# Attention and feed-forward on one Trainium2 core: three-product half-precision arithmetic replaced by an expansion about each batch's mean value

## The chip, the cores and the metric

The kernel runs on one core of one Trainium2 chip. The metric is the device time of one execution in microseconds (us), the median over runs. Engines are named as in the profile: PE (matrix products), PEld (its weight loads), DVE (vector), ACT (scalar and table functions), POOL (GpSimd) and SP (here only the queue from which all transfers are issued).

## The reference

```python
B, N, C = 4, 12288, 128            # kv: (4, 384, 32, 128), w_sr: (128, 128)
kv_pool = kv.reshape(B, 96, 4, 8, 4, C).mean(axis=(2, 4))     # 768 keys a batch, means of 16 places
k = v = kv_pool.reshape(B, 768, C) @ w_sr
s = (q @ k.transpose(0, 2, 1)) / sqrt(C)
a = exp(s - s.max(-1)); a /= a.sum(-1) + 1e-9
x = (a @ v).reshape(49152, 128)
h = x @ w_in                        # 128 -> 2048
out = (h - tanh(h)) @ w_out         # 2048 -> 128
```

All arrays are float32 but the two feed-forward weights, which are float64 and are handed over as pairs of 32-bit words. q is drawn with a standard deviation of 0.8, kv with 0.1 and w_sr with 0.05.

## The kernel before

The 49,152 tokens are cut into 96 groups of 512 (`NG` = 24 groups for each of 4 batches). Features lie on the 128 partitions, tokens on the free axis. Every piece of work is an operation of a `Plan`: it has a step (a priority), an engine, an assumed duration, and the tiles that it reads and writes. `Plan.run` places all operations by a list schedule and emits them in that order, so each engine's instruction order is fixed when the kernel is built. Tables of numbers (`SHIFT`, `FIRST`, `EARLY`) move the steps of each kind of operation. An added dependency, commented as "the shared way", puts a POOL instruction behind the DVE instruction emitted just ahead of it.

- `weights_in`, `weights_out` and `words_of` turn the float64 words into float32, and then into high and low half-precision parts (`wih`, `wil`, `woh`, `wol`, `wos`).
- `keys` makes a batch's 768 keys. For batch 0 PE sums the 16 places by accumulating products; for later batches DVE reduces chunks `kc` in pieces (L541).
- `attention` for a group: q is split in a high and a low half, PE multiplies three pairs of halves into `s` (L738, four blocks of 128 tokens by 768 keys), DVE takes the row maximum (L746), ACT the exponential (L752) and a half-precision copy (L757), POOL the remainder `a` (L761). A transposing DMA turns the weights, PE multiplies three pairs again (L819, 18 products of 512 columns), and DVE divides by the sum of the row (L833), which went through DRAM.
- `feed_forward` for a group: eight units `u` of 256 features. For each, PE makes `h` in three half-precision products for each of two halves (L860 to L862), ACT takes tanh (L888) and its square (L891), DVE multiplies `h` by it (L894). POOL, or ACT for unit 3, takes the high half `gh` (L898, L902), DVE the low half `gl` (L905), and PE goes back in three products for each half (L866 to L868) into the bank `acc`. So tanh itself is evaluated at one point of a quadrature for each value, and h - tanh(h) comes from it.
- `is_small` checks limits under which this holds. If they don't, a branch at the end (`ffn_any`) computes everything again for any inputs.
- `busy` fills pauses at the start with spare products (L1159).

PSUM has eight banks of 512 float32: `s` takes two, `h` two pairs, `x` and `acc` one each.

Of the kernel before, what the change touches and what calls it, by code (L numbers as in the profile page):

```python
# [9 lines left out]
F32 = mybir.dt.float32  # L10
I32 = mybir.dt.int32
U32 = mybir.dt.uint32
U16 = mybir.dt.uint16
BF16 = mybir.dt.bfloat16
F16 = mybir.dt.float16
# [4 lines left out]
DRAM = bass.MemoryType.DRAM  # L20
# [5 lines left out]

SMALL = 0.04
NODE = math.sqrt(0.6)
WEIGHT = math.sqrt(5.0 / 9.0)

# [9 lines left out]

LIFT = 15


SCORE = 2.0**20
MOST = 65000.0

LOW = 4096.0

LARGE, RAISE, LEAST = 30, 37, 2.0**11

ON_ACT = (3,)  # L60

IN_AFTER, OUT_AFTER = (0, 2, 4, 6), (8, 10, 12, 14)


SYNC = mybir.DependencyInfo(mybir.DependencyClass.Sync, mybir.DependencyReason.DATA)


class Plan:

    HOP = 0.1
    OWN = {"DVE": 0.16, "ACT": 0.02}

    SHIFT = {
        "divide": -1.31, "exps": -1.11, "forth": 0.78, "fro": 3.81, "g_high": 0.18,  # L80
        "g_low": 0.61, "inverse": -0.62, "largest_score": -1.19, "largest_x": -0.1,
        "load_row": 1.75, "load_words": -0.23, "pool": 14.11, "q_high": 0.01, "q_low": 0.58,
        "result": -1.34, "scores": 0.17, "square": -0.97, "store": -0.67, "store_row": 2.86,
        "store_x": -1.51, "tanh": -0.49, "turn_weights": -0.28, "values": 0.65,
        "weight_high": 3.21, "weight_low": 0.56, "x_high": 0.74, "x_low": -6.78,
    }

    FIRST = {
        "add": -1.15, "copy": -2.95, "copy_row": -3.44, "diagonals": 2.15, "divide": 2.2,
        "exps": -0.48, "forth": 3.21, "fro": 5.77, "g_high": 5.63, "g_low": -0.58, "high": 1.2,  # L90
        "inverse": 1.95, "keys_wide": -3.05, "largest": 1.58, "largest_score": -0.7,
        "largest_share": -0.86, "largest_x": -0.04, "load_q": -0.86, "load_row": 0.3,
        "load_words": 2.23, "low": 0.38, "lower": 1.13, "pool": 12.09, "q_high": -1.54,
        "q_low": 1.38, "result": 0.16, "rows": 0.22, "scaled": -0.24, "scores": -4.96,
        "scores_wide": -1.06, "shares": 2.06, "shift": -0.18, "size": -0.23, "sizes": 3.78,
        "small": 3.27, "square": -0.09, "squares_q": 3.77, "store": 0.64, "store_row": 3.52,
        "store_x": 1.91, "sum_of_rows": -1.91, "sums": 5.55, "tanh": 1.16, "times": 0.34,
        "top": -0.25, "turn_weights": 3.35, "upper": -0.01, "values": 1.54, "values_high": 0.24,
        "weight_high": -0.71, "weight_low": 3.46, "whole": 0.51, "within": 0.38, "x_high": -1.77,
        "x_low": -3.93,  # L100
    }
    UNTIL = 28
    SOON_FIRST, FIRST_US = 0.111, 150.0

    EARLY = {"attention 0": -5.7, "attention 1": 10.0, "attention 2": 2.9, "attention 3": 2.0, "weights_in": 3.9, "weights_out": 7.1}
    KEEP_US = 75.0
    SOON = 0.153
    TURN = 0.19

    def __init__(self, tc):  # L110
        self.tc = tc
        self.ops, self.tiles, self.rings = [], {}, {}
        self.names, self.later, self.emitted = {}, [], set()

    def tile(self, key, tag, bufs, make):
        ring = self.rings.setdefault(tag, [])
        self.tiles[key] = dict(make=make, ring=ring, place=len(ring), bufs=bufs, by=[], ap=None)
        ring.append(key)
# [7 lines left out]
    def op(self, step, engine, us, emit, reads=(), writes=(), late=0.0, port=False, dma=0.0,  # L126
           name=None, after=None, wide=False, dram=None):

        i = len(self.ops)
        kind = getattr(emit, "func", emit).__name__
# [1082 lines left out]
```

## Time and profile before

| | |
|---|---|
| median of 3 runs | 2829.96 us (2829.03 to 2830.73) |
| span of the profiled execution, first to last instruction | 2827.8 us |
| what lies around that span, against the median | 2.2 us |
| matrix products, weight loads | 13444 each |
| DVE, ACT, POOL instructions | 3201, 3311, 1057 |
| DMA | 285.02 MB, mean 101 GB/s |
| granted clock of PE, mean over the span | 1.000 |

The page gives the share of the span in which each engine was busy, then the same in 40 slices, then groups of instructions with the mean duration of one. A duration of DVE or ACT reaches a little into the next instruction of the same engine, so two neighbours' starts are closer together than the duration says. A matrix product's duration contains the way through the array, so products that follow one another start much closer together than their durations. For both the timeline, which gives each start, is read beside the groups.

### The profile page before, as it was taken

The numbers are of one execution on the slowest core, as the hardware profiler recorded it, in microseconds if no ns is written. First come the engines' busy times: TensorE is split into PE (matmuls) and PEld (weight loads), VectorE is DVE, ScalarE is ACT, GpSimd is POOL, SyncE is SP. The second block draws the span as 40 slices with busy tenths as digits, with TensorE's granted clock in tenths as the row PEclk, the third lists the DMA queues.
The fourth block names the chain that finished last, engine by engine and source line by source line (L and its number), as shares of the span: only waits on it lengthen the run. The fifth ranks groups of instructions, "written<-read, shape, count | busy, mean of one in ns | idle before, by whom it ended". The sixth has DMA issues, their size and how long they took to land. (4 is left out here: it accounts for less than half of the span.)

```text
span 2827.8 us, 39636 instructions
## 1 busy us (share of the span) xinstructions
PE 2791.7 (99%) x13444; PEld 1318.1 (47%) x13444; DVE 2693.8 (95%) x3201; ACT 2606.8 (92%) x3311; POOL 1327.6 (47%) x1057
## 2 busy tenths in 40 slices
PE   7999999999999999999999999999999999999998
PEld 4444444444444444444444444444444444444443
DVE  7999999999999999999999999999999999999998
ACT  7999999999999999999999999999999999999987
POOL 1545444444445454444445454444445454545442
PEclk9999999999999999999999999999999999999999
DMA  8534455554444445555434444555444444444440
GB/s 235 107 73 99 94 114 118 109 119 88 91 94 94 93 94 120 118 117 101 98 85 94 93 94 101 116 118 115 103 94 89 91 93 92 94 94 94 90 83 24
DMA packets 700324, 285.02 MB, mean 101 GB/s; under 512 B 629072, under 2 KB 656848, under 8 KB 700112
## 3 DMA queue, kind: packets, MB, share of 16 engines
q1 hardware_dynamic: 700112, 282.41, 46.8%
q8 instruction: 107, 1.75, 0.3%
q14 instruction: 105, 0.86, 0.1%
HBM read 79.23 MB, written 50.52 MB: 46 GB/s over the span
## 5 line engine op out<-in xcount | busy, mean ns | idle before, releaser
L898 POOL TENSOR_SCALAR gh<-gg 128x1024 f16<-128x1024 f32 x672 | 701.2, 1043 | 1344.0 <-DVE gl L905 1038.0
L894 DVE SCALAR_TENSOR_TENSOR gg<-h,by_batch,t 128x1024 f32<-128x1024 f32 x768 | 978.0, 1274 | 23.7 <-ACT t L891 17.3
L905 DVE SCALAR_TENSOR_TENSOR gl<-gh,gg 128x1024 f16<-128x1024 f16 x768 | 969.2, 1272 | 1.5 <-POOL gh L898 0.2
L888 ACT ACTIVATE t<-h,by_batch 128x1024 f32<-128x1024 f32 x768 | 849.6, 1106 | 63.4 <-PE h L862 55.2
L891 ACT ACTIVATE t<-t 128x1024 f32<-128x1024 f32 x768 | 811.4, 1056 | 21.0
L761 POOL TENSOR_TENSOR a<-e,a 128x768 f16<-128x768 f32 x380 | 625.8, 1647 | 147.0 <-ACT a L757 74.4
L860 PE MATMUL h<-x,wih 128*128 128x512 f16 x1536 | 582.7, 379 | 11.5 <-DVE gg L894 11.0
L868 PE MATMUL acc<-gl,wos 128*128 128x512 f16 x1536 | 582.1, 379 | 1.3 <-DVE gl L905 1.3
L861 PE MATMUL h<-x,wih 128*128 128x512 f16 x1536 | 582.1, 379 | 0.9 <-DVE x L840 0.9
L866 PE MATMUL acc<-gh,woh 128*128 128x512 f16 x1536 | 582.1, 379 | 0.3 <-POOL gh L898 0.2
L867 PE MATMUL acc<-gh,wol 128*128 128x512 f16 x1536 | 582.1, 379 | 0.0
L862 PE MATMUL h<-x,wil 128*128 128x512 f16 x1536 | 582.1, 379 | 0.0
L819 PE MATMUL x<-at,vv 128*128 128x512 f16 x1728 | 466.0, 379 | 2.2 <-DVE xf L833 1.7
L752 ACT ACTIVATE e<-s,nm 128x768 f32<-128x768 f32 x380 | 340.7, 897 | 98.0 <-DVE nm L748 60.5
L746 DVE TENSOR_REDUCE nm<-s 128x1 f32<-128x768 f32 x380 | 360.3, 948 | 43.7 <-PE s L738 43.3
L757 ACT CAST a<-e 128x768 f16<-128x768 f32 x384 | 316.3, 825 | 4.9
L738 PE MATMUL s<-vt,qh 128*128 128x384 f16 x1520 | 309.1, 326 | 3.1 <-ACT e L752 2.0
L819 PEld LDWEIGHTS <-vv 128*128 128x128 f16 x1728 | 169.0, 98 | 203.5 <-issue 3.0
L860 PEld LDWEIGHTS <-wih 128*128 128x128 f16 x1536 | 149.9, 98 | 217.0 <-DVE gg L894 51.9
L862 PEld LDWEIGHTS <-wil 128*128 128x128 f16 x1536 | 150.3, 98 | 182.3 <-issue 1.2
L868 PEld LDWEIGHTS <-wos 128*128 128x128 f16 x1536 | 150.3, 98 | 181.2
L861 PEld LDWEIGHTS <-wih 128*128 128x128 f16 x1536 | 150.3, 98 | 170.8 <-issue 5.7
(141 smaller groups left out, 1848.4 us busy)
## 6 DMA issues: line engine op xcount, KB each, us to landing
qs<-in_q_dram SPq DMA_DIRECT2D x96, 256.0 KB, 3.2
xs<-x SPq DMA_DIRECT2D x96, 256.0 KB, 2.4
out_dram<-o SPq DMA_DIRECT2D x96, 256.0 KB, 2.7
row<-sums_row SPq DMA_DIRECT2D x94, 256.0 KB, 4.0
kc<-in_kv_dram SPq DMA_DIRECT2D x36, 512.0 KB, 4.6
at<-a SPq DMA_TRANSPOSE x384, 3.8
kc<-in_kv_dram SPq DMA_DIRECT2D x8, 384.0 KB, 7.7
words<-in_moe_w_in_dram SPq DMA_DIRECT2D x4, 512.0 KB, 8.7
```

Source lines behind the costliest of these rows:

```text
L761: return on.tensor_tensor(out=plan[a][:, 1], in0=plan[e], in1=plan[a][:, 0], op=ALU.subtract)
L819: PE.matmul(out=plan[x], lhsT=l, rhs=r, start=(n == 0 and k == 0), stop=(n == KT - 1 and k == 2))
L860: PE.matmul(out=h, lhsT=wih[:, fs], rhs=xh, start=True, stop=False)
L861: PE.matmul(out=h, lhsT=wih[:, fs], rhs=xl, start=False, stop=False)
L862: PE.matmul(out=h, lhsT=wil[:, fs], rhs=xh, start=False, stop=True)
L866: PE.matmul(out=acc, lhsT=woh[:, fs], rhs=gh, start=(f == 0), stop=False)
L868: PE.matmul(out=acc, lhsT=wos[:, fs], rhs=gl, start=False, stop=(f == FT - 1))
L888: A.activation(out=plan[t], in_=plan[h], func=AF.Tanh, scale=node)
L891: A.activation(out=plan[t], in_=plan[t], func=AF.Square)
L894: V.scalar_tensor_tensor(out=plan[gg], in0=plan[h], scalar=weight, in1=plan[t], op0=ALU.mult, op1=ALU.mult)
L898: return PL.tensor_scalar(out=plan[gh], in0=plan[gg], scalar1=1.0 / LOW, scalar2=1.0, op0=ALU.mult, op1=ALU.mult)
L905: return V.scalar_tensor_tensor(out=plan[gl], in0=plan[gh], scalar=-LOW, in1=plan[gg], op0=ALU.mult, op1=ALU.add)
```

## The change

The new kernel keeps the groups, the plan and the units. What it computes differs.

- **Attention.** The mean of the 768 keys is taken out of keys and values (`mean`, `apart`, `centre`). Then x is that mean `cen` plus a remainder. With r2 = exp(s) - 1 - s, the remainder is (scale/K) times the moment matrix of the values times q (`Mn`, linear, a float32 product of 128x128 by 512) plus the values times r2, divided by 1 + mean(r2). r2 comes from one ACT exponential and one DVE instruction on tiles of 128 keys by two key blocks of 512 tokens. The keys lie on the partitions now, so nothing is transposed, no maximum is taken and no row of sums goes through DRAM. `shares` adds r2 over the keys by a product with a constant matrix, `share_left` takes 1 away.
- **Feed-forward.** About h0 = w_in^T cen, h - tanh(h) is expanded: a constant `G0`, a linear term `A` (float32 product per token, matrix made once a batch), and a second and third order term u^2 (1 + u), where u is the scaled deviation of h. `winr` and `Wr` carry the scales of each feature. Six units of eight are ACT `square` and DVE `cube`; two (`ON_POOL`, units 0 and 3) are an ACT copy and three POOL instructions.
- All other products take operands of type float32r with one instruction for each 512 columns; q and the deviation `dl` are rounded to it by POOL (L580, L635).
- Keys of batches 1 to 3 are added up by POOL in four folds a chunk (L356), those of batch 0 by DVE for eight chunks (L362) and POOL for four.
- A group takes 50 float32r products and 2 float32 products on PE, 9 DVE instructions of 1024 and 2 of 512 elements, 11 ACT instructions of 1024 and 1 of 512, and on POOL 2 + 4 instructions of 1024 and 2 of 512.
- The tables `SHIFT`, `FIRST` and `EARLY`, the spare products and "the shared way" are gone. PSUM: `big`, three pairs of banks for scores and `h` alike, and `x` and `acc`.
- `fits` checks limits for this expansion; if they don't hold, the branch `any_inputs` computes all again.

POOL in the middle of the program, before (a run of remainders `a` and high halves `gh`):

```order
L761 TENSOR_TENSOR a<-e,a 128x768
L898 TENSOR_SCALAR gh<-gg 128x1024 x2
L761 TENSOR_TENSOR a<-e,a 128x768
L898 TENSOR_SCALAR gh<-gg 128x1024
L761 TENSOR_TENSOR a<-e,a 128x768
L898 TENSOR_SCALAR gh<-gg 128x1024 x3
```

POOL in the middle of the program, now (`z` and `rp` are the two units' work from the copy `v`, `dr` and `qr` the rounded deviation and q, `kc` and `kvp` a fold of keys):

```order
L687 TENSOR_TENSOR rp<-z,v 128x1024
L356 TENSOR_TENSOR kc<-kc 128x64x4
L356 TENSOR_TENSOR kc<-kc 128x64x2
L356 TENSOR_TENSOR kc<-kc 128x64x8
L635 TENSOR_SCALAR dr<-dl 128x512
L683 TENSOR_SCALAR z<-v 128x1024
L687 TENSOR_TENSOR z<-z,v 128x1024
L687 TENSOR_TENSOR rp<-z,v 128x1024
L580 TENSOR_SCALAR qr<-q 128x512
```

The remainders and high halves are gone; a fold, the two roundings and chains of three instructions, each reading what the one ahead wrote, stand in their place.

PE in the middle of the program, before (products of the feed-forward, each with a weight load of its own):

```order
L866 MATMUL acc<-gh,woh 128x512
L867 LDWEIGHTS wol
L867 MATMUL acc<-gh,wol 128x512
L868 LDWEIGHTS wos
L868 MATMUL acc<-gl,wos 128x512
L860 LDWEIGHTS wih
L860 MATMUL h<-x_10645,wih 128x512
```

PE in the middle of the program, now (float32r products load their weights themselves; L619 is the float32 product with `Mn`):

```order
L669 MATMUL big<-dr,winr 128x512 x4
L709 MATMUL acc<-r,Wr 128x512 x2
L619 MATMUL x<-q,Mn 128x512
L669 MATMUL big<-dr,winr 128x512 x2
L624 MATMUL x<-r_6803,vvr 128x512 x2
L709 MATMUL acc<-r,Wr 128x512 x2
L595 MATMUL big<-qr,kTr 128x512 x2
L624 MATMUL x<-r_6864,vvr 128x512 x2
```

One product stands where three stood, and attention's products are mixed in between pairs of the feed-forward's.

PE at the start of the program, now (the batch's matrices from `Wg` and `winT`, the constant from `hb`, then the first scores):

```order
L460 MATMUL big<-col,win_65 128x1 x16
L526 MATMUL big<-Wg,winT 128x128 x16
L495 MATMUL big<-hb,wout_67 128x1 x4
L548 MATMUL big<-Wg,winT 128x128 x4
L495 MATMUL big<-hb,wout_67 128x1 x4
L548 MATMUL big<-Wg,winT 128x128 x4
L495 MATMUL big<-hb,wout_67 128x1 x4
L548 MATMUL big<-Wg,winT 128x128 x4
L495 MATMUL big<-hb,wout_67 128x1 x4
L548 MATMUL big<-Wg,winT 128x128 x4
L595 MATMUL big<-qr,kTr 128x512 x8
```

The first scores stand behind all float32 products of batch 0, which wait for the weights of both layers. On POOL, six of the twelve chunks of batch 1, and half of the seventh, are folded ahead of the first unit's `z`.

The core of the diff (what is removed is printed above):

```diff
+R32 = mybir.dt.float32r
-    SHIFT = {
-        "divide": -1.31, "exps": -1.11, "forth": 0.78, "fro": 3.81, "g_high": 0.18,
...
 def keys(b, s0):
+            if b or j % 3 == 2:
+                for k, w in enumerate((8, 4, 2, 1)):
+                    def fold(key=key, w=w, at=at):
+                        x = plan[key]
+                        to = plan[kvp][:, at].unsqueeze(2) if w == 1 else x[:, :, 0:w]
+                        PL.tensor_tensor(out=to, in0=x[:, :, 0:w], in1=x[:, :, w : 2 * w], op=ALU.add)
...
+def about_centre(b, s0):
+            plan.op(s1 + j * by / 2, "DVE", 0.72, diagonal, (hb, "ident"), (dg,), port=True)
+            plan.op(s1 + j * by / 2, "PE", 0.9, scaled, (dg, "winT"), ((pw, k),), late=0.2)
...
+            plan.op(s3 + n / 4, *(("POOL", 1.15) if b else ("DVE", 0.72)), by_first,
+                    (hb, ("wout32", n)), (wg,), port=True)
+            plan.op(s5, "PE", 0.9, slopes, (wg, "winT"), (pa,), late=0.2)
+            plan.op(s4 + n / 4, "POOL", 1.15, by_third, (hb, ("wout32", n)), ((Wr, n),))
...
 def attention(g, s0):
+        def rounded_q():
+            PL.tensor_scalar(out=plan[qr], in0=plan[qs], scalar1=1.0, scalar2=1.0, op0=ALU.mult,
+                             op1=ALU.mult)
+            def scores(k=k, s=s):
+                for h in range(2):
+                    n = 2 * k + h
+                    PE.matmul(out=half(plan[s], h), lhsT=plan[kTr][:, n * P : (n + 1) * P],
+                              rhs=plan[qr], start=True, stop=True)
+            def exps(s=s, e=e):
+                A.activation(out=plan[e], in_=plan[s], func=AF.Exp)
+            def beyond(s=s, e=e, r=r):
+                V.scalar_tensor_tensor(out=plan[r], in0=plan[e], scalar=-1.0, in1=plan[s],
+                                       op0=ALU.add, op1=ALU.subtract)
+        def shares(k):
+            for h in range(2):
+                PE.matmul(out=plan[den], lhsT=share, rhs=half(plan[f"r2.{g}.{k}"], h), ...
+        def straight():
+            PE.matmul(out=plan[num], lhsT=plan[Mn], rhs=plan[qs], start=True, stop=False)
+        def values(k):
+            for h in range(2):
+                PE.matmul(out=plan[num], lhsT=plan[vvr][:, n], rhs=half(plan[f"r2.{g}.{k}"], h), ...
+        def share_left():
+            V.tensor_scalar(out=plan[t], in0=plan[den], scalar1=1.0, scalar2=None,
+                            op0=ALU.subtract, op1=ALU.max, accum_out=most[:, g : g + 1])
+        def apart():
+            V.tensor_tensor(out=plan[dl], in0=plan[num], in1=plan[t], op=ALU.mult)
+        def rounded():
+            PL.tensor_scalar(out=plan[dr], in0=plan[dl], scalar1=1.0, scalar2=1.0, ...
...
+    ON_POOL = (0, 3)
 def feed_forward(g, s0):
+        def straight():
+            PE.matmul(out=plan[acc], lhsT=plan[Am], rhs=plan[dl], start=True, stop=False)
+            def forth(n=n, hp=hp):
+                for h in range(2):
+                    f = 2 * n + h
+                    PE.matmul(out=half(plan[hp], h), lhsT=plan[winr][:, f * P : (f + 1) * P],
+                              rhs=plan[dr], start=True, stop=True)
+            def square(hp=hp, u=u):
+                A.activation(out=plan[u], in_=plan[hp], func=AF.Square)
+            def cube(hp=hp, u=u, r=r):
+                V.scalar_tensor_tensor(out=plan[r], in0=plan[hp], scalar=1.0, in1=plan[u],
+                                       op0=ALU.add, op1=ALU.mult)
+            def copy(hp=hp, v=v):
+                A.copy(out=plan[v], in_=plan[hp])
+            def moved_pool(v=v, z=z):
+                PL.tensor_scalar(out=plan[z], in0=plan[v], scalar1=1.0, scalar2=1.0,
+                                 op0=ALU.add, op1=ALU.mult)
+            def times(to, x, y):
+                PL.tensor_tensor(out=plan[to], in0=plan[x], in1=plan[y], op=ALU.mult)
+            if n in ON_POOL:
+                plan.op(s, "ACT", 1.06, copy, (hp,), (v,), late=0.1)
+                plan.op(s, "POOL", 1.05, moved_pool, (v,), (z,))
+                plan.op(s, "POOL", 2.2, partial(times, z, z, v), (z, v), (z,))
+                plan.op(s, "POOL", 2.2, partial(times, r, z, v), (z, v), (r,))
+                back_at = s + 5
+            def back(n=n, r=r):
+                for h in range(2):
+                    f = 2 * n + h
+                    PE.matmul(out=plan[acc], lhsT=plan[Wr][:, f], rhs=half(plan[r], h), ...
...
+    start(-LEAD - 80)
+    weights(-LEAD - 50, -LEAD - 60)
     for b in range(B):
+        keys(b, first - LEAD - (60 if b else 40))
+        about_centre(b, first - LEAD - (40 if b else 30))
         for g in range(b * NG, (b + 1) * NG):
+            attention(g, g * UN - LEAD)
```

More of the change, by code (lines that the diff above doesn't have):

```diff
@@ L77 @@
     OWN = {"DVE": 0.16, "ACT": 0.02}
-    SHIFT = {
-        "divide": -1.31, "exps": -1.11, "forth": 0.78, "fro": 3.81, "g_high": 0.18,
[L81 to L108, printed above, removed]
+    SOON = 0.15
     def __init__(self, tc):
@@ L1151, in skip_is_likely @@
         tc.no_sync_barrier()
-    def busy(times):
-        for tag in ("x", "acc"):
-            begun = [k for k in plan.rings[tag] if plan.tiles[k]["ap"] is not None]
-            if not begun or plan.over(begun[-1]):
-                spare = ps.tile([P, G], F32, tag=tag, name="spare", bufs=1)
-                for _ in range(times):
-                    PE.matmul(out=spare[:, 0:P], lhsT=wsr, rhs=wsr, start=True, stop=True)
-                return
-    plan.busy = busy
     plan.run(skip_is_likely)
```

1187 lines of the change are left out of this document (493 added, 694 removed).

## The prediction

> **What bounds the kernel now.** I read the engines' busy shares first, then the slices, the groups by line, and the timeline, since several engines look full.
>
> ```profile
> span 2827.8 us, 39636 instructions
> PE 2791.7 (99%) x13444; PEld 1318.1 (47%) x13444; DVE 2693.8 (95%) x3201; ACT 2606.8 (92%) x3311; POOL 1327.6 (47%) x1057
> PE   7999999999999999999999999999999999999998
> POOL 1545444444445454444445454444445454545442
> PEclk9999999999999999999999999999999999999999
> ```
>
> PE is full from the second slice to the last but one, at full clock; POOL is half empty. The timeline of PE gives the pace of its products, and that of float32 beside it.
>
> ```profile
> 1443.32 0.38 PE L866 MATMUL acc<-gh,woh 128*128 128x512 f16 x1
> 1443.53 0.38 PE L867 MATMUL acc<-gh,wol 128*128 128x512 f16 x1
> 1443.75 0.38 PE L868 MATMUL acc<-gl,wos 128*128 128x512 f16 x1
> ...
> 20.70 0.81 PE L552 MATMUL s<-gl,wsr 128*128 128x384 f32 x2
> 21.35 0.81 PE L552 MATMUL s<-gh,wsr 128*128 128x384 f32 x2
> ...
> 32.67 3.29 PE L1159 MATMUL spare<-wsr 128*128 128x128 f32 x28
> ```
>
> A half-precision product of 512 columns starts every 0.215 us, whatever its duration of 0.38. A group takes 18 + 96 of those and 24 of 384 columns (0.16): 114 x 0.215 + 24 x 0.16 = 28.4 us, and 96 groups 2722 us. That is the time before. A float32 product of 384 columns stands as two rows, and one starts every 0.65 us: 0.65/384 = 1.69 ns a column, four times 0.215/512 = 0.42. Its weight loads hide behind it. Products of 128 columns come at 3.29/28 = 0.118 us a row, 0.235 each.
>
> **The change on PE.** A group now has 50 float32r products and 2 in float32 (512 x 1.69 ns = 0.865 us). No row shows float32r. Its bounds are the nearest rows: 0.215 us as half precision, 0.865 as float32, and between them 0.43, since a float32 row alone takes two passes' time. I take 0.215: one instruction for each product, with no split into halves, is what half precision has. Then a group is 50 x 0.215 + 2 x 0.865 = 12.5 us. By the Trainium skill (FP8 and Floating Point Precision, section TensorE Precision Notes) true float32 is four passes, high and low parts of both operands, and a reduced precision reads the four bytes and truncates; the four passes agree with the 1.69 ns above, one pass would cost 0.215 us; by it rivals 3 and 4 below, to which the rows leave 0.09, would be out, and no run before this change shows it. Each batch adds float32 matrices: keys and values 0.65 x 2 + 6 x 0.235, moments 6 x 0.235, 32 of 128 columns (7.5 us) and 32 of one column (0.235 at most each, 7.5 us): 19 us. PE in all: 96 x 12.5 + 3 x 19 = 1257 us after the start.
>
> **DVE and ACT.** The groups with their durations, and neighbours' starts:
>
> ```profile
> L894 DVE SCALAR_TENSOR_TENSOR gg<-h,by_batch,t 128x1024 f32<-128x1024 f32 x768 | 978.0, 1274 | 23.7 <-ACT t L891 17.3 <-PE h L862 1.7
> L888 ACT ACTIVATE t<-h,by_batch 128x1024 f32<-128x1024 f32 x768 | 849.6, 1106 | 63.4 <-PE h L862 55.2
> L898 POOL TENSOR_SCALAR gh<-gg 128x1024 f16<-128x1024 f32 x672 | 701.2, 1043 | 1344.0 <-DVE gl L905 1038.0 <-PE acc L868 190.5 <-PE s L738 29.5
> L761 POOL TENSOR_TENSOR a<-e,a 128x768 f16<-128x768 f32 x380 | 625.8, 1647 | 147.0 <-ACT a L757 74.4 <-ACT t L888 28.9 <-ACT qj L718 7.8
> L927 ACT ACTIVATE o<-acc,by_batch 128x512 f32<-128x512 f32 x96 | 64.3, 670 | 6.2 <-PE acc L868 6.2
> L492 DVE TENSOR_TENSOR o<-o,acc 128x512 f32<-128x512 f32 x2 | 1.3, 682 | 0.0
> L358 DVE TENSOR_SCALAR ym<-ym 128x512 f32<-128x512 f32 x8 | 3.4, 422 | 10.6 <-ACT ym L355 10.6
> ...
> 1422.54 1.27 DVE L894 SCALAR_TENSOR_TENSOR gg<-h,by_batch,t 128x1024 f32<-128x1024 f32 x1
> 1423.74 0.94 DVE L746 TENSOR_REDUCE nm<-s 128x1 f32<-128x768 f32 x1
> ...
> 1427.01 1.06 ACT L891 ACTIVATE t<-t 128x1024 f32<-128x1024 f32 x1
> 1427.97 0.81 ACT L757 CAST a<-e 128x768 f16<-128x768 f32 x1
> 1428.69 1.11 ACT L888 ACTIVATE t<-h,by_batch 128x1024 f32<-128x1024 f32 x1
> 1429.83 1.06 ACT L891 ACTIVATE t<-t 128x1024 f32<-128x1024 f32 x1
> ```
>
> `beyond` and `cube` read one operand from PSUM and one from SBUF over 1024 elements, as L894 does. Its start is followed by the next after 1.20 us, not 1.27. `share_left` and `apart` are near L492, 0.68 less the same 0.08. A group on DVE: 9 x 1.20 + 2 x 0.60 = 12.0 us. On ACT the overlap is 0.10 (L891: 1.06, next start after 0.96); 11 instructions between 0.96 and 1.01 (L888 less the overlap) and the result at 0.57: 11.7 us. L888 to L891 takes 1.14, because L891 reads what L888 wrote: an instruction that waits for its own engine's last one costs ACT some 0.13 us more.
>
> **POOL is the new bound.** Each of two units is one instruction like L898 (1.043) and two with two operands; L761 gives 1.647/768 = 2.145 ns an element, 2.20 us for 1024. The two roundings are half of L898. POOL's own timeline has no overlap but a gap of 0.08:
>
> ```profile
> 1402.43 1.04 POOL L898 TENSOR_SCALAR gh<-gg 128x1024 f16<-128x1024 f32 x1 [2.38 <-PE acc L867]
> 1403.55 1.65 POOL L761 TENSOR_TENSOR a<-e,a 128x768 f16<-128x768 f32 x1
> 1405.29 1.04 POOL L898 TENSOR_SCALAR gh<-gg 128x1024 f16<-128x1024 f32 x1
> ...
> 1420.18 1.30 DVE L840 TENSOR_TENSOR x<-xf,x 128x512 f16<-128x512 f32 x1
> ```
>
> A group: 2 x (1.12 + 2 x 2.28) + 2 x 0.60 = 12.55 us, x 96 = 1205. A chunk of keys is four folds of 512 + 256 + 128 + 64 elements, 960 x 2.145 ns + 4 x 0.08 = 2.38 us; 6.5 of the 36 chunks fall into the start, 29.5 cost 70 us. `by_first` and `by_third` of three batches are 24 x (512 x 2.145 ns + 0.08) = 28 us. Waits for POOL's own last result: six in a group and four in a chunk, 694. The trace has none on POOL, so their price lies between 0 (its rows don't overlap, the result is nearly there) and ACT's 0.13: 0 to 90 us; I take the middle of a smaller half, 0.06, or 42 us, because POOL already pays 0.08 without such a wait. Sum 1345 us: 14.4 us a group while keys are folded, 12.9 in the last batch. The Trainium skill (GPSIMD Engine Reference, section 3.1 Elementwise) advises against such work on GpSimd and gives 4497 ns for an addition of 2048 float32 elements; half of that, an estimate of 2.25 us, would make the 384 instructions 20 us dearer, and the forecast at the end 1446 for 1426.
>
> The other three need 13.3 us or less a group while POOL needs 14.4, so what waits for POOL (ACT's `copy` for a free `v`, PE's products from `rp`, and the queues behind them) waits within that slack. In the last batch PE's 12.5 is close to 12.9. Two nearly full engines in fixed order wait for each other; no row prices it, between nothing and the whole difference to their sum, and I add 0.5 us for 24 groups, 12 us. PSUM: one of three pairs is held 0.43 for the products, 0.17 until they land, about 1.1 on ACT and 1.3 on DVE: 3.0 us for nine tiles and 1.7 for two, 30.4/3 = 10.1 us a group, below the bound.
>
> A DVE instruction with two SBUF operands was held by POOL (L840 above took 1.30 beside a POOL instruction, against a usual 0.68). In the loop after, all of DVE's eleven read one operand from PSUM, like L894, so I charge nothing for that. What covers it is PSUM as the source; `diagonal`, four a batch, is not covered and costs at most 4 x 0.62 us, which lies within DVE's spare time.
>
> **Start and end.**
>
> ```profile
> 0.00:5.00 5.00, 0.00 (x0) 0.00 (x0) 0.41 (x3) 1.28 (x1) 0.53 (x5) 1.00 0.55 171
> 5.00:20.00 15.00, 14.45 (x37) 7.73 (x37) 8.54 (x15) 6.10 (x10) 0.00 (x0) 1.00 1.02 376
> 20.00:37.00 17.00, 14.62 (x72) 10.15 (x72) 14.54 (x34) 12.59 (x23) 0.00 (x0) 1.00 0.78 287
> ...
> 2819.53 1.23 DVE L905 SCALAR_TENSOR_TENSOR gl<-gh,gg 128x1024 f16<-128x1024 f16 x1
> ...
> 1414.32 0.15 DVE L642 TENSOR_SCALAR by_batch<-by_batch 128x1 int32<-128x1 int32 x1
> 1414.51 0.15 DVE L644 TENSOR_SCALAR by_batch<-by_batch 128x1 f32<-128x1 f32 x1
> ```
>
> The first load is the same: 4.2 MB of weights, 6.3 of keys and 1 of q, and the windows' rates bring 11.4 MB by 37 us; w_out is last, at about 35. Its last decoding takes 2.5. Then DVE does 22 small dependent instructions of `coefficients` (a start every 0.19 us: 4.2) and eight of 0.61 for the matrices (4.9), PE the last four products (1): 48 us. Behind these stand the first scores: products, exponential, three `beyond`, `shares`, `share_left`, `values`, `apart`, rounding, `forth` and the copy add 12. POOL's first unit starts at 60 us. At the end, `back`, result and store follow its last; from DVE's last instruction before to the end were 2827.8 - 2820.8 = 7 us.
>
> Sum: 60 + 1345 + 12 + 7 = 1424 us of span, and with the 2.2 us that lie between span and median 1426.
>
> **The rivals.**
>
> 1. PE binds, not POOL: own waits on POOL cost nothing and its two-operand instructions are shorter than in proportion. Then 60 + 1257 + 12 + 7 + 2 = 1338. For it: the proportion rests on a single length. Against: POOL's 1205 + 98 is above 1257 even with free waits. Chance 0.12.
> 2. The hand-overs are worse: waits at 0.13 (48 us more), folds with their runs of 8, 4 and 2 elements 1.5 times as long (30), half a microsecond more on the 72 other groups (36): 1540. For it: every engine is above four fifths full, with a fixed order laid out for other durations. Chance 0.13.
> 3. float32r takes 0.43 us: PE 50 x 0.43 + 1.73 = 23.2 us a group, 96 x 23.2 + 57 + 69 = 2353. For it: the only 4-byte rows take twice the half-precision time each. Chance 0.06.
> 4. The other side: float32r costs as float32, 0.865 us. PE 45 us a group, 96 x 45 + 126 = 4446, slower by 57%. It decides from (2827.8 - 126)/96 = 28.1 us a group, or 0.53 us a product. Against it: float32's 0.865 is two rows of 0.43 each, for operands of full length, and these are rounded to fewer bits first. Chance 0.03.
> 5. The limits of `fits` don't hold and the branch runs. A unit there has some twenty DVE instructions of 512 elements, each at least 0.42 (L358): 20 x 0.42 x 16 x 96 = 12,900 us at least. The drawn spreads give scores of standard deviation 0.8 x 0.025 x 0.05 x 11.3 = 0.0113, and so mean(r2) near 6.4e-5; the largest token may double it, and the limit is 2^-12 = 2.4e-4. Chance 0.02.
>
> **How the numbers follow.** The forecast has 0.64, at 1426. A range of 1335 to 1550 takes in rivals 1 and 2, and leaves out 3 to 5 (0.11) and what lies beyond these bounds (0.07). A measurement tells some 0.2% from no change; only 4 and 5 are slower, 0.05, nothing aims at no change (0.01), and faster has 0.94.
>
> **What would show it.** POOL busy above 85% and full in the slices up to the last quarter, the other engines at 80 to 92%. Rows: float32r products starting every 0.215 us; `times` at 2.2 us, `cube` and `beyond` near 1.27; the first `z` near 60 us. The prediction is wrong if PE's products start further apart, if POOL shows idle time that ends by PE or DVE, or if `times` is well off 2.2.

## The result and the profile after

The changed kernel takes 1651.41 us (median of 4 runs, 1650.85 to 1654.81) against 2829.93 us: a ratio of 0.584, 95% interval 0.583 to 0.5847. That is faster, and 225 us above the forecast, outside its range. The page of the changed kernel, in the lines that were shown of before, and the chain that ended last by engine:

```profile
span 1649.7 us, 17651 instructions
PE 1477.3 (90%) x5902; PEld 1052.3 (64%) x5902; DVE 1235.3 (75%) x1353; ACT 1116.8 (68%) x1204; POOL 1375.5 (83%) x961
PE   4798999989899999997999999999999999999996
POOL 4599888799998888879998888887878888888886
PEclk9799999989999999999999999999999999999998
POOL 64%; PE 18%; issue 6%; ACT 6%; DVE 3%; DMA 1%; SPq 0%; POOLq 0%; ACTq 0%; DVEq 0%
```

POOL carries the chain, as forecast, but it is 83% busy and not full, above all in the last quarter, where it has the least to do. The groups by line (busy time and mean ns, then idle time before them) and the table of waits name what it exchanges waits with:

```profile
L676 DVE SCALAR_TENSOR_TENSOR r<-big,u 128x1024 fp32r<-128x1024 f32 x576 | 688.3, 1219 | 143.5 <-ACT u L673 134.4
L687 POOL TENSOR_TENSOR z<-z,v 128x1024 f32<-128x1024 f32 x192 | 459.7, 2394 | 15.9
L687 POOL TENSOR_TENSOR rp<-z,v 128x1024 fp32r<-128x1024 f32 x192 | 459.0, 2391 | 15.1
L683 POOL TENSOR_SCALAR z<-v 128x1024 f32<-128x1024 f32 x192 | 201.9, 1051 | 127.8 <-ACT v L680 125.7
...
PEld acc L709 <- POOL rp L687: 151.4, 169, 3.5
POOL z L683 <- ACT v L680: 125.7, 76, 4.7
```

PE stands before products that need POOL's `rp`, and POOL before `z`, which needs ACT's copy of what PE made. The chain of waits in the middle shows this as one loop (start, duration, what):

```profile
1005.48 2.42 POOL rp L687
1007.90 0.04 issue
1007.94 0.73 PE acc L709 x2
1008.67 0.47 PE big L669 x2
...
1009.23 1.02 ACT v L680
...
1010.39 1.05 POOL z L683
...
1016.34 0.64 POOL qr L580
```

`rp` ends at 1007.90. PE's next instructions, in fixed order, are the two products from `rp`; only then comes the pair of products for the unit that POOL takes next; ACT copies it, and POOL starts at 1010.39. Of these 2.49 us POOL fills 0.62 with the rounding `dr`; the rest it idles, once a group. The `qr` of the group before started at 1001.28, this one at 1016.34: 15.06 us a group, where POOL's own work is 13.2 (two units of 1.13 + 2.47 + 2.42 by their starts, and two roundings of 0.57).

Time by stretches of the program (from the starts of `o`, L715, one a group; the first of the four columns is the prediction's):

| us a group | forecast | changed kernel | POOL's durations corrected (e5_pool_costs) | TensorE nearly alone (e13_pe_first) |
|---|---|---|---|---|
| first 12 groups | 14.35 | 15.93 | 14.74 | 14.14 |
| 8 groups around each change of batch | 14.35 | 19.32, 19.16, 18.18 | 17.98, 18.20, 17.89 | 16.49, 16.70, 16.64 |
| 16 groups between changes, twice | 14.35 | 15.37, 15.27 | 14.15, 14.15 | 13.91, 13.91 |
| last 25 | 13.4 | 15.20 | 13.83 | 13.86 |
| span | 1424 | 1649.7 | 1544.1 | 1477.2 |

The forecast's 14.35 is its 12.55 + 42/96 and its 98 us of keys and matrices over 72 groups; 13.4 its 12.9 for the last batch and the 0.5 for two full engines. The start came later too: the first `z` (81.22) instead of 60.

```profile
40.00:60.00 20.00, 13.57 (x73) 13.52 (x74) 17.43 (x38) 5.22 (x8) 10.05 (x9) 0.55 0.12 40
81.22 1.06 POOL L683 TENSOR_SCALAR z<-v 128x1024 f32<-128x1024 f32 x1
```

In the first row (columns PE, PEld, DVE, ACT, POOL, granted clock, DMA share, GB/s) the clock granted to PE is 0.55 on average, and 0.50 from 38 to 57.5 us, while the matrices of batch 0 are made one from the other. The forecast counted these products at the full clock. The Trainium skill (TensorE: Matmul & The Clock Gate, Part 1) says that the gate passes half of the pulses until TensorE has been busy for about 3.4 us. The half agrees with the 0.50; the 3.4 us do not show here, since the clock stayed at 0.50 through the 32 one-column rows of L460, which are marked busy from 39.07 to 45.90.

### The profile page after: what moved, and what is told of

It is laid out like the page before. It is cut to its first block, busy times and chain, and to the rows that moved or that the text cites. A ratio compares the mean times of both kernels' runs of the same rounds, so it can differ in the third digit from the quotient of the medians.

```text
span 1649.7 us, 17651 instructions
## 1 busy us (share of the span) xinstructions
PE 1477.3 (90%) x5902; PEld 1052.3 (64%) x5902; DVE 1235.3 (75%) x1353; ACT 1116.8 (68%) x1204; POOL 1375.5 (83%) x961
## 4 chain that ended last, share of the span: by engine, by line
POOL 64%; PE 18%; issue 6%; ACT 6%; DVE 3%; DMA 1%; SPq 0%; POOLq 0%; ACTq 0%; DVEq 0%
POOL z L687 25%; POOL rp L687 22%; POOL z L683 11%; PE acc L709 7%; ACT v L680 5%; PE big L669 4%; POOL qr L580 3%; POOL kc L356 2%; PE x L624 1%; PE big L460 1%; PE x L615 1%; PE big L595 1%; PE big L526 1%; PE x L619 1%; PE big L495 1%
## 5 line engine op out<-in xcount | busy, mean ns | idle before, releaser
L676 DVE SCALAR_TENSOR_TENSOR r<-big,u 128x1024 fp32r<-128x1024 f32 x576 | 688.3, 1219 | 143.5 <-ACT u L673 134.4
L673 ACT ACTIVATE u<-big 128x1024 f32<-128x1024 f32 x576 | 576.1, 1025 | 197.3 <-PE big L669 197.1
L669 PE MATMUL big<-dr,winr 128*128 128x512 f32 x1536 | 500.4, 426 | 37.3 <-DVE r L602 28.9
L602 DVE SCALAR_TENSOR_TENSOR r<-E,big 128x1024 fp32r<-128x1024 f32 x288 | 350.1, 1216 | 178.8 <-ACT E L599 178.0
L687 POOL TENSOR_TENSOR z<-z,v 128x1024 f32<-128x1024 f32 x192 | 459.7, 2394 | 15.9
L687 POOL TENSOR_TENSOR rp<-z,v 128x1024 fp32r<-128x1024 f32 x192 | 459.0, 2391 | 15.1
L669 PEld LDWEIGHTS big<-dr,winr 128*128 128x128 f32 x1536 | 282.1, 190 | 170.1 <-DVE r L602 68.5
L599 ACT ACTIVATE E<-big 128x1024 f32<-128x1024 f32 x288 | 296.3, 1029 | 119.7 <-PE big L595 111.8
L709 PE MATMUL acc<-r,Wr 128*128 128x512 f32 x1152 | 363.0, 400 | 1.1 <-DVE r L676 1.1
L683 POOL TENSOR_SCALAR z<-v 128x1024 f32<-128x1024 f32 x192 | 201.9, 1051 | 127.8 <-ACT v L680 125.7
L709 PEld LDWEIGHTS acc<-r,Wr 128*128 128x128 f32 x1152 | 218.5, 191 | 50.6 <-DVE r L676 2.0
L709 PEld LDWEIGHTS acc<-rp,Wr 128*128 128x128 f32 x384 | 60.1, 192 | 153.3 <-POOL rp L687 151.4
L619 PE MATMUL x<-q,Mn 128*128 128x512 f32 x192 | 98.9, 596 | 1.0 <-DVE t L628 1.0
```

Source lines behind the costliest of these rows:

```text
L599: A.activation(out=plan[e], in_=plan[s], func=AF.Exp)
L602: V.scalar_tensor_tensor(out=plan[r], in0=plan[e], scalar=-1.0, in1=plan[s], op0=ALU.add, op1=ALU.subtract)
L669: PE.matmul(out=half(plan[hp], h), lhsT=plan[winr][:, f * P : (f + 1) * P], rhs=plan[dr], start=True, stop=True)
L673: A.activation(out=plan[u], in_=plan[hp], func=AF.Square)
L676: V.scalar_tensor_tensor(out=plan[r], in0=plan[hp], scalar=1.0, in1=plan[u], op0=ALU.add, op1=ALU.mult)
L683: PL.tensor_scalar(out=plan[z], in0=plan[v], scalar1=1.0, scalar2=1.0, op0=ALU.add, op1=ALU.mult)
```

## The experiments

Three theories were on record before the first four runs. Theory 1: the fixed order was laid out with assumed durations that are too short for POOL, so the engines wait for one another. Theory 2: POOL's work alone, at its longer duration, fills the time. Theory 3: TensorE's own pace and stalls set the period, whatever the order. All runs with a ratio were timed beside the kernel before.

**paces.** One operation after another, alone or beside another engine.

> Computes no part of the reference: rows of products and of POOL instructions, each kind alone, to price the two kinds of instruction that came out dearer than forecast. PE: 48 float32r products each of 512, 384, 256 and 128 columns, the same 512 with one weight matrix only, 24 float32 and 48 half-precision products. If the weight load sets float32r's pace (theory A), 512 columns start every 0.23 us and 384 columns no faster than 0.23; if the columns set it (theory B), 384 columns start every 0.17 and 512 every 0.215 when nothing else runs. POOL: products of two operands of 1024 elements. If the operands' type makes the difference to the 2.20 us scaled from 768 elements (theory C), float32 with float32 takes 2.39 with DVE idle and float32 with half precision 2.20; if DVE beside it does (theory D), it takes 2.20 to 2.25 alone and 2.39 beside a DVE that reads PSUM and SBUF. Beside a DVE that reads SBUF twice both engines should be slower, DVE by 1 us or more.

The timeline of PE (two float32r products a row, then two in half precision) and the groups by shape (the second row of L82 gives the shortest, median and longest of its durations in ns):

```profile
31.36 0.62 PE L46 MATMUL one<-qr 128*128 128x512 f32 x2
31.81 0.61 PE L46 MATMUL two<-qr 128*128 128x512 f32 x2
...
69.44 0.59 PE L46 MATMUL two<-qh 128*128 128x512 f16 x2
69.87 0.59 PE L46 MATMUL one<-qh 128*128 128x512 f16 x2
...
L82 DVE SCALAR_TENSOR_TENSOR dv<-qf 128x1024 f32<-128x1024 f32 x24 | 55.6, 2319 | 0.8
L84 POOL TENSOR_TENSOR pf<-x,y 128x1024 f32<-128x1024 f32 x12 | 39.3, 3305 | 0.1
L82 DVE SCALAR_TENSOR_TENSOR dv<-qf x24: 1218/3242/3246, 139.8 to 195.0; 128x1024 f32<-128x1024 f32 x24
L74 DVE SCALAR_TENSOR_TENSOR dv<-pair,qf 128x1024 f32<-128x1024 f32 x24 | 29.4, 1224 | 0.8
L62 POOL TENSOR_TENSOR pf<-x,y 128x1024 f32<-128x1024 f32 x12 | 27.8, 2356 | 6.5 <-DMA y<-in_q_dram 6.5
L76 POOL TENSOR_TENSOR pf<-x,y 128x1024 f32<-128x1024 f32 x12 | 27.7, 2352 | 0.1
L66 POOL TENSOR_TENSOR ph<-x,qh 128x1024 f16<-128x1024 f32 x12 | 25.1, 2127 | 0.0
L68 POOL TENSOR_TENSOR ph<-x,qh 128x768 f16<-128x768 f32 x12 | 19.2, 1636 | 0.0
```

Float32r takes 0.2265 us a product (0.453 a pair), 5% more than half precision (0.43 a pair), and not a multiple of it. At 384 columns it takes 0.1735, so the columns set its pace and not the weight load. POOL's product of two float32 operands takes 2.356 us alone and 2.352 beside a DVE instruction that reads PSUM (L76, L74): no contention. With one operand and the result in half precision it takes 2.127, and 1.636 at 768 elements, which is the kind of row that the forecast scaled from (1.647). So that row was the wrong kind: the types make 2.36 out of 2.13, where scaling by length had given 2.20. Whether the operand or the result does it, these rows do not separate. A DVE instruction that reads SBUF twice and POOL's product slow each other. POOL's takes 3.305; DVE's mean of 2.319 mixes 13 rows beside POOL, of 3.24 each, with 11 rows outside of it, of 1.22. The eleven DVE instructions of a group hold none of this kind, but `diagonal` (L520), four a batch, is one.

**e1_costs, e2_slack, e3_one.**

```diff
 e1_costs: every assumed duration as the trace shows it, e.g.
-plan.op(s, "POOL", 2.2, partial(times, r, z, v), (z, v), (r,))
+plan.op(s, "POOL", 2.48, partial(times, r, z, v), (z, v), (r,))
-plan.op(at, "DVE", 1.27, beyond, (s, e), (r,), late=0.08)
+plan.op(at, "DVE", 1.14, beyond, (s, e), (r,), late=0.08)
 e2_slack:
-plan.op(s, "POOL", 2.2, partial(times, r, z, v), (z, v), (r,))
+plan.op(s, "POOL", 2.2, partial(times, r, z, v), (z, v), (r,), late=2.5)
 e3_one:
-ON_POOL = (0, 3)
+ON_POOL = (0,)
```

> The same instructions; the durations that the plan assumes are set to what the profile measured (POOL 1.13 and 2.48 for 1.05 and 2.2, ACT 0.92 for 1.06, DVE 1.14 for 1.27, PE 0.46 for 0.44 and so on), so only the order changes. Theory 1 (order): once a group POOL's result is waited for by PE, the product for POOL's next unit stands behind that wait, then ACT's copy, then POOL again; some 2.4 us of every 15.3 are exposed because POOL was assumed faster than it is. Then the order for true durations hides most of it: 1500 to 1570 us. Theory 2 (POOL's work alone): POOL is short of time by its own dearer instructions and any order ends the same: 1630 us or more. Theory 3 (PE's pace with stalls): also 1620 or more.

1544.61 us, ratio 0.5457 (0.5448 to 0.5466). The same instructions in another order save 107 us. POOL is 89% busy, and the two waits of the loop fall from 151.4 and 125.7 to 19.5 and 26.8 us.

> One number changed: the plan is told that POOL's last instruction of a unit lands 2.5 us later than it does, so that PE's products from it move back in PE's order and the products for POOL's next unit stand ahead of them. All durations assumed as before. Theory 1: POOL's waits for ACT's copy (126 us) and PE's waits for POOL (231 us with the weight loads) nearly vanish: 1510 to 1580. Theory 2 and 3: 1630 or more; with a result slower than before if the bank of the accumulator, held longer, is what binds.

1581.92 us, ratio 0.5592 (0.5583 to 0.5601): slack behind POOL's last instruction alone brings 70 of the 107. The two waits fall to 25.6 and 27.1 us; the time is 2 us above theory 1's bounds.

> One unit of eight goes through POOL, not two; the other goes to ACT and DVE. POOL falls to some 7.5 us a group, DVE rises to 13 us. Theories 1 and 2: POOL's loop is no longer the longest thing, and PE (50 x 0.232 + 2 x 0.93 = 13.5 us a group) or DVE set the time: 1400 to 1470. Theory 3: 1600 or more, since PE keeps all its products.

1631.79 us, ratio 0.5764 (0.5755 to 0.5774). POOL is down to 50% and the time hardly moves: a miss for theory 1 as I had put it, and for theory 2. In its chain, between one `rp` and ACT's next copy stand 7.7 us of PE's products in fixed order, and the loop is as long as before. By its number it speaks for theory 3; e1 speaks against it.

**e4_one_costs, e5_pool_costs, e6_r32.** The edits are e1's durations and e3's single unit together; POOL's durations alone, with two units; and e4 with the two float32 products in float32r.

```diff
 e6_r32, beside e4_one_costs:
-PE.matmul(out=plan[num], lhsT=plan[Mn], rhs=plan[qs], start=True, stop=False)
+PE.matmul(out=plan[num], lhsT=plan[Mn], rhs=plan[qr], start=True, stop=False)
-PE.matmul(out=plan[acc], lhsT=plan[Am], rhs=plan[dl], start=True, stop=False)
+PE.matmul(out=plan[acc], lhsT=plan[Am], rhs=plan[dr], start=True, stop=False)
```

(A group has eight units; the "five" in these three texts is wrong.)

> One unit of five on POOL, as in the run with one unit, and in addition every assumed duration of the plan set to what the trace of the changed kernel shows. Theory 1 (the fixed order, laid out with durations that were too short, leaves each engine waiting for the one before it): TensorE is then the bound, 96 groups x 13.5 us (50 float32r products x 0.232 and 2 float32 ones x 0.93) = 1292, with 81 before the first group's POOL work, some 57 for the folds and phase changes and 10 behind it: 1440 to 1490 us. Theory 3 (TensorE's pace with its stalls sets the period whatever the order): at least 1540 us, since the TensorE work is the same as in every run so far. Theory 2 (POOL's work alone): POOL is half empty here, so it gives no bound above 1440.

1607.71 us, ratio 0.5677 (0.5667 to 0.5688): theory 1 missed again.

> Two units of five on POOL as in the changed kernel; only POOL's assumed durations in the plan are set to what the trace shows (the 1024-column product 2.48 us, the one from ScalarE's rows 1.13, the 0.59 of the small ones, the folds, the first batch's coefficients); ScalarE's and VectorE's stay as they were. If POOL's too short durations alone made the order bad, most of the 107 us that all corrected durations brought comes back: 1540 to 1575 us. If ScalarE's and VectorE's matter as much: 1620 us or more.

1543.34 us, ratio 0.5451 (0.5441 to 0.5461), as fast as e1. POOL's durations are the whole of the effect.

> One unit of five on POOL, all durations of the plan as measured, and the two float32 products of each group (the linear terms by the small matrices) made float32r, so that their operands are rounded more coarsely: TensorE falls from 13.5 to 52 x 0.232 = 12.1 us a group. Theory 1: VectorE (12.7 us a group with its extra unit) becomes the bound, 96 x 12.7 = 1219 with the same 150 us around it: 1360 to 1420 us. Theory 3 (stalls beside the products): 1450 us or more. If it takes as long as the run with one unit and measured durations, TensorE was not the bound of that run.

1514.99 us, ratio 0.5352 (0.5343 to 0.5362): 93 us less than e4, so PE's time is on e4's path, yet the run is above the expected 1420. e4's chain shows what stands beside the products:

```profile
1012.22 0.48 PE acc L709 x2
...
1013.31 1.02 ACT u L673
...
1014.36 1.24 DVE r L676
...
1015.64 0.72 PE big L669 x2
```

PE waits for a PSUM pair that `cube` gives back, and a pair of products behind a wait takes 0.72 instead of 0.46.

**e7_half, e8_alternate, e9_alternate_r32.**

```diff
 e7_half, in e4's order (cube the same way; back reads the first half twice):
-A.activation(out=plan[u], in_=plan[hp], func=AF.Square)
+A.activation(out=half(plan[u], 0), in_=half(plan[hp], 0), func=AF.Square)
 e8_alternate, with e1's durations (e9: with e6's products too):
-if n in ON_POOL:
+if n in ((0,), (0, 3))[g % 2]:
```

> The run with one unit and measured durations took 1607.71 us; in its trace TensorE's row is nearly always marked busy, yet a group takes 15.3 us where its 50 float32r and 2 float32 products are 13.0 to 13.5 us of work. This run keeps that order on every engine, and all of TensorE's work, and halves what ScalarE and VectorE do for the seven units a group that are not on POOL (512 of 1024 columns; the second projection reads the first half twice, so the other half of these units' values is left out). Theory 1, made narrower: TensorE stands before units whose PSUM buffer ScalarE and VectorE have not yet given back (three such buffers, eleven units a group): with these waits gone a group takes 13.0 to 13.5 us and the run 1400 to 1460 us. Theory 3 (the extra time is TensorE's own, in its products or in the loading of weights): 1560 us or more. In between: both.

1533.96 us, ratio 0.5424 (0.5411 to 0.5437): in between, 74 us below e4.

> All durations of the plan as measured; POOL takes two units of eight in every second group and one in the others (the earlier texts said of five: it is eight units a group). POOL's work falls from 14.4 to some 11.3 us a group, VectorE's is 12.2, TensorE's 13.0 to 13.5. Theory 1: POOL no longer binds as in the run with two units and measured durations (1544.61 us), and fewer PSUM buffers wait for VectorE than with one unit (1607.71 us): 1480 to 1540 us. Theory 3: no better than with two units, 1540 to 1610 us.

1569.42 us, ratio 0.5544 (0.5534 to 0.5553), in theory 3's bounds. Its groups take 13.6 and 15.6 us in turn, though.

> As the last one, and the two float32 products of a group made float32r (their operands are rounded more coarsely): TensorE 12.1 us a group, VectorE 12.2, POOL 11.3. With one unit on POOL this change of the products gave 1514.99 us, 93 us less. Theory 1: 1400 to 1470 us. Theory 3: 1440 to 1520 us, a like 93 us below the run before it.

1477.47 us, ratio 0.5219 (0.5205 to 0.5232), the fastest of all runs with the whole work, with the coarser rounding; just above theory 1's bounds, within theory 3's.

**e10_hop, e11_best.** The plan learns that a wait before a product costs more.

```diff
-HOP = 0.1
+HOP, TO_PE = 0.1, 0.35   # TO_PE for operations on PE
```

> Two units of eight on POOL, all durations of the plan as measured (1544.61 us so far), and one number more: the plan lets TensorE's work begin 0.35 us after what it waits for instead of 0.1, since in the traces two products behind a wait take 0.73 us against 0.46 for two without one. Nothing else differs. Theory 1, with the waits before TensorE's products as what is left: a group without batch work falls from some 13.9 to 14.8 us towards TensorE's 13.5, and the run takes 1490 to 1530 us. If what is left is not a matter of the order: 1540 us or more.

1556.21 us, ratio 0.5496 (0.5485 to 0.5508): 12 us slower than e1.

> The fastest run so far (1477.47 us: POOL takes two units and one in turn, all products float32r with the small matrices' operands rounded more coarsely, durations as measured) with the same 0.35 us before TensorE's work in the plan. Its groups take 11.6 and 15.4 us in turn, 13.5 on average, where TensorE has 12.1 and VectorE 12.2 us of work. Theory 1: 12.7 to 13.2 on average, 1390 to 1445 us. If the order is not what is left: 1470 us or more.

1495.17 us, ratio 0.5279 (0.5268 to 0.529): 18 us slower than e9. Both miss: telling the plan that a wait before PE's products costs 0.35 us does not mend what is left.

**e12_pe, e13_pe_first, e14_pool_pe.** To separate TensorE's own time from its waits, nearly everything else was emptied while each order stayed.

```diff
 e12_pe (e4's order), e13_pe_first (the changed kernel's): all of exps, beyond, square, cube, copy, moved, times, e.g.
-A.activation(out=plan[u], in_=plan[hp], func=AF.Square)
+A.activation(out=few(plan[u]), in_=few(plan[hp]), func=AF.Square)   # 128 of 1024 columns
-rhs=half(plan[r], h)
+rhs=again(plan[r])                                                 # those 128, four times
 e14_pool_pe (e5's order): the same outside of POOL's units
```

> The order of the run with one unit on POOL and measured durations (1607.71 us), with all of TensorE's work, while ScalarE, VectorE and POOL handle 128 of 1024 columns in every unit and every exponential (the other columns' work is left out; TensorE reads the 128 columns repeatedly). If TensorE's time there was waiting for the other engines: a group of 13.0 to 13.5 us, and the run 1400 to 1460 us, with the weights, the batch changes and the end as before. If TensorE itself takes 15.3 us a group in this program (theory 3): 1560 us or more.

1509.22 us, ratio 0.5335 (0.5326 to 0.5344), between both expectations.

> The same emptying of ScalarE, VectorE and POOL (128 of 1024 columns) in the changed kernel's own order, two units on POOL, durations of the plan as they were (1651.41 us with the full work). If waiting: 1400 to 1460 us again, whatever the order. Theory 3: 1560 us or more.

1476.45 us, ratio 0.521 (0.5201 to 0.5219), 16 us above the bounds for waiting and 84 below theory 3's. The chain of one group, in which TensorE is nearly all that is left:

```profile
1303.11 0.47 PE acc L715 x2
...
1303.60 0.70 ACT o L721
...
1304.34 1.13 PE acc L664 x2
1305.47 0.47 PE big L601 x2
1305.94 0.47 PE x L621 x2
1306.41 0.93 PE acc L715 x4
1307.35 0.93 PE big L675 x4
1308.28 0.86 PE x L625 x2
...
1318.28 1.13 PE acc L664 x2
```

From one `acc L664` to the next are 13.94 us. 25 pairs of float32r products at 0.465 and two float32 ones at 0.86 make 13.35. The rest is the exchange of the one bank `acc`: its first product waits until ACT has read the last group's result, and takes 1.13 behind that wait instead of 0.86 (0.27), and the wait of 0.76 hides one pair (0.30 left). 13.35 + 0.57 = 13.92. e12's order stands a second time in the same way, before the one bank `x` (DVE's `share_left`), and takes 14.44. That the single banks cost this was read from the chain; with eight banks in use no run could double them.

> The order of the run with two units and only POOL's durations corrected (1543.34 us), with POOL's work and TensorE's whole, and ScalarE and VectorE at 128 of 1024 columns outside POOL's units. If POOL and TensorE by themselves hold that run: no better than 1520 us. If the waits for VectorE and ScalarE are what is left above TensorE's 13.5 us a group: 1440 to 1500 us.

1521.72 us, ratio 0.5376 (0.5364 to 0.5388): 22 us below e5, not the 43 or more that would have made VectorE and ScalarE the cause. The windows over the last 25 groups, changed kernel, e5, e14 in this order (busy PE, PEld, DVE, ACT, POOL):

```profile
1234.98:1614.98 380.00, 355.03 (x1350) 245.55 (x1351) 295.11 (x299) 281.34 (x301) 320.17 (x198) 1.00 0.10 32
```

```profile
1162.39:1508.23 345.84, 340.71 (x1348) 249.11 (x1348) 292.19 (x299) 281.73 (x300) 321.07 (x198) 1.00 0.11 36
```

```profile
1150.05:1486.00 335.95, 334.25 (x1346) 250.84 (x1345) 97.02 (x298) 125.69 (x299) 319.55 (x197) 1.00 0.11 37
```

The same number of products takes 380, 346 and 336 us, 15.20, 13.83 and 13.44 a group. The last is all but TensorE's 13.35. So TensorE can run this program at its spacing, and theory 3 falls in its strong form; what an order adds to 13.35 is waits. Theory 2 falls with e1, which has the same POOL work as the changed kernel.

## Why the prediction was wrong

**What held.** POOL carries the chain; float32r runs at nearly half precision's pace, and rivals 3 and 4 are out. With POOL's durations corrected, the groups between changes take 14.15 us with POOL at 13.6 to 13.7 busy, where 14.35 was forecast for POOL as the bound. That these two are so close is in part luck: TensorE nearly alone takes 13.91 in these groups (e13), where 13.3 was counted. DVE (1.13 us between neighbours' starts) and ACT (0.92) were below the forecast, and DVE's reading of PSUM beside POOL cost nothing, as charged.

**The step that failed** is "what waits for POOL ... waits within that slack". It took POOL's sum as the period because the other engines had a microsecond or more to spare on average. But each engine's order is fixed by the plan, and there POOL's product stood with 2.2 us where it takes 2.39 and a gap of 0.08. So each `rp` comes later than the order expects; PE's queue stands before it, holding up the products that POOL's next unit needs, and POOL then waits for what it has itself delayed. Of the 225 us, the order is 107 (e1 against the changed kernel, the same instructions). The second rival was this in kind, "a fixed order laid out for other durations", at a chance of 0.13; it was priced at half a microsecond for 72 groups, 36 us.

**The other 118 us** remain with the order mended. They are read from the stretches of e5 and its trace, against the forecast's terms:

- The start: 81 instead of 60, 21 us. By the changed kernel's chain, 8 of them lie ahead of `coefficients`, which begin at 45.9 where the forecast's terms give 37.5. Another 10 lie between these and the first scores (65.9), because the products L526, L495 and L548 stand on PE one behind another from 52.3 on, where the forecast charged the last four products. The other 3 lie behind. The halved clock is an estimated 6 of the 21: the 32 rows of L460 take 6.6 us and those of L526 6.4, while eight and sixteen of them take 0.79 and 1.80 in e5 at a later change of batch.
- The changes of batch: 24 groups take 18.0 us where 14.35 was forecast, 88 us. The forecast spread the batch's work evenly over 24 groups of POOL. In fact most of it falls into eight groups, where TensorE nearly alone needs 16.6 (e13, in the changed kernel's order), which makes 54 of the 88; an average over the batch hid that the bound changes there. VectorE's and ScalarE's unit work makes some 5 (e14: 17.67, 17.97 and 17.74). POOL's folds, some of which fall into these groups, do not explain the rest: at the third change, with no further batch to fold, POOL is busy for 14.2 us a group instead of 16.0 and 16.3, and a group takes 17.89 all the same. The trace of e5 at the first change shows what else the forecast left out:

```profile
341.51 3.58 DVE L520 TENSOR_TENSOR Wg<-ident,hb 128x512 f32<-128x512 f32 x3
341.68 4.31 POOL L553 TENSOR_TENSOR Wr<-wout,hb 128x512 fp32r<-128x512 f32 x3 [0.32 <-DVE hb L491]
346.27 3.79 PE L526 MATMUL big<-Wg,winT 128*128 128x128 f32 x16 [5.66 <-DVE r L676]
353.48 1.95 PE L526 MATMUL big<-Wg,winT 128*128 128x128 f32 x16
```

Ahead of L526 PE stands idle for 5.66 us. DVE works meanwhile through 22 small instructions that depend on one another (334.3 to 341.6), then through three of `diagonal`, 1.2 us each beside POOL's L553 where the fourth takes 0.68, and only then does the `cube` (L676) that PE waits for. The forecast had put `diagonal` into DVE's spare time. Behind the pause the clock granted to PE is 0.50 (346 to 350), and the same sixteen rows take 3.79 instead of 1.95; over these stretches of e5 it is 0.95, 0.95 and 0.98. At the third change the pause is 1.46. No run takes these parts from one another.

- The other 44 groups of the first three batches are 0.04 us below, -2 us; the last 25 are 0.43 us above, 11 us. There TensorE is the bound and not POOL: 13.35 us a group where 12.5 was forecast, since a float32r product takes 0.2325 in the loop (0.465 a pair) against the assumed 0.215.

These sum to 118; the span of e5, 1544.1, is 120 above 1424.

**Terms that were off and cancelled in part.** POOL's 384 products took 2.39 instead of 2.20, 73 us more. In return the price of waiting for POOL's own last result, 42 us, was nothing, so that by its starts POOL's work is 13.2 us a group where 12.9 was forecast: the gap to a dependent instruction is 0.07 to 0.08 us, the same 0.08 that was already charged, and the short instructions overlap their neighbours by 0.04. From the 4497 ns that the Trainium skill (GPSIMD Engine Reference, section 3.1 Elementwise) gives for an addition of 2048 elements, the estimate was 2.25 us for such a product; the 2.356 of paces is 5% above it, and the 2.20 that I scaled from a row lies further off.

**What stays open.** With one unit of eight on POOL and measured durations a group takes 15.30 us although no engine's own work is above 13.5. Of the 1.8 us above that, half of ScalarE's and VectorE's unit work accounts for 0.8 (e7: 14.46), and TensorE in that order takes 14.44 when all else is nearly free (e12). Why the plan finds no better order there, and none when it is told of the 0.35 us, was not settled.

The best version with the same arithmetic is the changed kernel with POOL's durations corrected, 1543.34 us; with coarser rounding in the two linear products and POOL's second unit in every other group, 1477.47.

## What to carry to other kernels

Where a program's order is fixed ahead by assumed durations, an engine near its limit whose work is assumed too short costs more than its own excess, because its late results hold up the very work that feeds it; correct the durations from a trace before judging the bound. Sum each engine by stretches of the program, not by averages, since work that is done once a batch can fall into a few groups and change the bound there; follow its chain of dependent steps too, since the other engines stand behind it in their fixed orders. Behind a wait a product cost some 0.27 us more than in a run here, so a single-buffered accumulator can show up as a fixed price for each group.

## What was not expected of the hardware

- A float32r product of 512 columns starts every 0.2265 us in a run and 0.2325 in the loop, half precision every 0.215; at 384, 256 and 128 columns it is 0.1735, 0.12 and 0.112, so below 256 columns hardly less.
- POOL's product of 1024 elements depends on its operands: 2.356 us for two in float32, 2.127 with one of them and the result in half precision.
- A DVE instruction with two SBUF operands and POOL's product take 3.24 and 3.305 us side by side, against 1.22 and 2.356 alone. With one DVE operand from PSUM they take 1.224 and 2.352 side by side. The Trainium skill (SBUF — State Buffer, section "SBUF: two separate sides") says that a DVE operation with two SBUF inputs and a GpSimd operation that reads SBUF exclude each other from a shared port; the first pair of numbers agrees, and the second shows that PSUM as a source avoids it.
- The clock granted to PE can fall while PE is never marked idle: in e13 at the first change of batch it is 1.00 from 316 to 319 us and 0.50 from 322 to 325, with PE marked busy throughout both. The 32 rows of one-column products (L466) stand just ahead, in between other products, and behind them a pair of float32r products takes 0.85 instead of 0.465.
